# Attention and gated layer on one core: first pairs' scores on row halves of the array, leftover keys times V on row halves with one PSUM bank for each tile's output, and a re-tuned planner

## The chip, the core and the metric

The kernel runs on one core of a Trainium2 chip. The metric is the device time of one execution in microseconds (us). Most executions of one kernel agree within 0.3%.

## The reference, cut to what matters

```python
# q, k, v: [8 batches, 8 heads, 576 tokens, 64]; tau = 0.02
scores = scale * np.matmul(q, k.transpose(0, 1, 3, 2))
thresh = np.max(scores, axis=-1, keepdims=True) - tau
scores = np.where(scores >= thresh, scores, -1000000000.0)
attn = np.exp(scores - np.max(scores, axis=-1, keepdims=True))
attn = attn / (np.sum(attn, axis=-1, keepdims=True) + 1e-09)
x = np.matmul(attn, v)            # then [4608 tokens, 512]
gate = 1.0 / (1.0 + np.exp(-(x @ w_gate)))     # w_gate, w_val: [512, 1536]
out = (gate * (x @ w_val)) @ w_out             # w_out: [1536, 512]
```

## The kernel before

Two heads make a pair, and 32 visits (8 batches of 4 pairs) do the attention. 576 tokens are four tiles of 128 and 64 left over, so a visit has nine tiles of queries: four for each head and one (`l`) with the 64 leftover queries of both heads. For each tile, `tile_steps` (L580) makes the scores on TensorE in a PSUM tile `s` (L609), their negated maximum on VectorE (`st`, L616), the threshold (L625), the exponential on ScalarE (`p`, L630), and on VectorE the mask with the row sums (L633). `normalise` multiplies by the reciprocal on GpSimd (L667). `transpose` turns 4 x 128 keys of a tile by TensorE (`tp`, L678), and ScalarE copies them out (`pt`, L640). `leftover_keys` (L691) turns the 64 leftover keys of two tiles at once: `lk`, copied to `pl`, holds the leftover keys of the first tile in rows 0 to 63 and those of the second in rows 64 to 127.

`output` (L696) multiplies by V for two tiles at a time. One PSUM tile `av` takes both, 256 columns, and 64 more in the second output of a visit (the `l` tile). Head h writes rows h*64 to h*64+63, so two matmuls with 64 columns of weights each lie side by side in the array. For the leftover keys V stands twice in `vs`, once with zeros under it and once with zeros above it (blocks NJ and NJ+1), so that a 128-row matmul takes the one tile's half of `pl` alone. ScalarE copies `av` to `xf` (L721).

The first four visits (batch 0, `plain_scores`, L554) make their scores in full float32, one matmul of 128 rows for each half of the keys: the rows of both heads of K, and Q of one head with zeros in the rows of the other (`q0`). All later visits use a split in two parts that runs at the fast rate (`split_scores`, L515), for which halves are copied to `kd` and `qd` by DMA.

The rest is the gated layer ("moe"): matmuls `m` (L774) and `o` (L817) for the blocks of batches 0, 1 and 2, and after the attention the six blocks that are left, in pairs with sums of blocks (`qa`, `qb`, `qc` of L1016, `ra`, `rb`, `rc` of L1081; their inputs `xs_p` are made by L921, L924 and L929 from `xb`). Its weights are first converted (`convert`, L402): 24 blocks of the input weights and 12 of the output weights, each a DMA in, an absolute value on ScalarE, a clamp on GpSimd, three VectorE instructions (L442, L446, L452), a copy on ScalarE, a difference on GpSimd or VectorE (L470, L466), and a DMA out.

The order on every engine is worked out when the kernel is built, by a planner (`Plan.run`, L119). Each operation has an engine, a cost and a key, and an engine takes the ready operation with the smallest key. Attention has the number of its tile as key, conversions `CONV_IN` and `CONV_OUT` (start and step, in tiles), the gated layer's matmuls 1,000,000, so they fill what attention leaves. `LAG` is what the planner adds for an operation whose input comes from another engine. Tiles named `b` are four PSUM banks: `tp`, `lk` and `av` (class `att`) may hold three of them, and two once the gated layer has begun (`cap`, L372). An engine then runs its instructions in that order, and waits in place for what isn't ready. SyncE (SP) issues nearly all DMAs, in its order too.

Of the kernel before, what the change touches and what calls it, by code (L numbers as in the profile page):

```python
# [204 lines left out]
CONV_IN, CONV_OUT = (10, 1.5), (56, 3)  # L205
# [11 lines left out]
NPS = 4  # L217
# [15 lines left out]
THR_FIRST, THR_UNTIL, LK_UNTIL = "POOL", 72, 72  # L233
# [29 lines left out]
SUMS_IN, SUMS_OUT, SUM_KEY = {1: (0,), 2: (1,)}, {0: (0,), 1: (1,)}, 400  # L263
# [25 lines left out]
def kernel(  # L289
# [195 lines left out]
    class Visit:  # L485
# [17 lines left out]
        def prepare(self, lead):  # L503
# [50 lines left out]
        def plain_scores(self, key, n):  # L554
            b, hp, c0, c1 = self.b, self.hp, self.c0, self.c1
            WM = self.WM = c1 - c0
            kn = self.k1 = buf(("kn", "qn")[hp % 2], [P, SK], F32, f"kp{n}")
            op("SP", 1.2, key - 4, lambda: nc.sync.dma_start(out=kn.ap, in_=k[b, hp]), writes=[kn])
            W = 2 * WM + (2 * SL if self.with_left else 0)
            qn = self.q1 = buf("kd", [P, W], F32, f"qp{n}")  # L560

            heads = [(0,), (1,)] if n == "0_0" else [(0, 1)]
            for hs in heads:
                c = slice(hs[0] * WM, (hs[-1] + 1) * WM)
                op("SP", 0.9 * len(hs), key - 4, lambda hs=hs, c=c: nc.sync.dma_start(
                    out=qn.ap[:, c].rearrange("p (h c) -> p h c", h=len(hs)),
                    in_=q0[4 * b + hp, :, hs[0] : hs[-1] + 1, c0:c1],
                ), writes=[(qn, h) for h in hs])
# [3 lines left out]
            if len(heads) == 1:
                op("ACT", act(W), key, lambda: nc.scalar.activation(qn.ap, qn.ap, AF.Copy, scale=scale_t[:, 0:1]), writes=[qn])
                return
            for i, c in enumerate((slice(0, WM), slice(WM, 2 * WM), slice(2 * WM, W))):
                op("ACT", act(c.stop - c.start), key, lambda c=c: nc.scalar.activation(
                    qn.ap[:, c], qn.ap[:, c], AF.Copy, scale=scale_t[:, 0:1]
                ), writes=[(qn, i)])

    def tile_steps(vis, g, i, key):  # L580
# [24 lines left out]

        def scores():
            for m, (st, mv) in enumerate(steps):
                for c in range(2):
                    nc.tensor.matmul(  # L609
                        s.ap[:, c, :HALF], st(), mv(slice(k0 + c * HALF, k0 + (c + 1) * HALF)),  # L610
                        start=m == 0, stop=m == len(steps) - 1,
                    )

        op("PE", 0.98 if vis.plain_s else len(steps) * 2 * mm(HALF), key, scores, reads=reads, writes=[s], also=[g.p])
# [28 lines left out]
    class Group:  # L643
# [52 lines left out]
        def output(self, c, key):  # L696

            vis, pt, pl = self.vis, self.pt, self.pl
            last = self.tiles[0] != 0
            W = 2 * P + (SL if last else 0)  # L700
            av = buf("b", [P, W], F32, f"av{self.name}", "att")
            c0 = self.tiles[0] * P

            ms = [(0, 2 * P, j, lambda h, j=j: pt.ap[:, h, j]) for j in range(NJ)]
            ms += [(i * P, (i + 1) * P, NJ + i, lambda h: pl.ap[:, h]) for i in range(2)]
            if last:
                sl = lambda h: slice(h * SL, (h + 1) * SL)
                ms += [(2 * P, W, j, lambda h, j=j: c.pt.ap[:, 0, j, sl(h)]) for j in range(NJ)]
                ms += [(2 * P, W, NJ + 1, lambda h: c.pl.ap[:, 0, sl(h)])]

            def go():
                for i, (a, z, j, m) in enumerate(ms):
                    for h in range(2):
                        nc.tensor.matmul(  # L714
                            av.ap[h * D : (h + 1) * D, a:z], vis.vs.ap[:, j, h], m(h),
                            start=i == 0, stop=i == len(ms) - 1, skip_group_check=True,
                        )
# [506 lines left out]
def _laid_out(inputs):  # L1224
# [16 lines left out]
    first = _np.zeros((NPS, 2, d, 2, m), q.dtype)  # L1241
    pairs = q.reshape(b * h // 2, 2, d, s)
# [54 lines left out]
```

## Time and profile before

| what | us |
|---|---|
| median of 3 runs (1376.15, 1377.9, 1383.55) | 1377.9 |
| the profiled execution's own time | 1375.02 |
| its span, first to last instruction | 1373.2 |
| TensorE (PE) busy | 1332.4 (97%) |
| VectorE (DVE) busy | 982.3 (72%) |
| ScalarE (ACT) busy | 708.8 (52%) |
| GpSimd (POOL) busy | 639.0 (47%) |

The page has groups of instructions by line, `out<-in`, with the mean time of one; the views of the trace give the same for a stretch of time, the waits between engines, and the instructions in order of time. A float32 matmul stands there as two records. Three stages are to be told apart: the attention of batch 0 with the first conversions (up to about 123 us), attention with the gated layer's matmuls between (up to 837 us), and the gated layer alone.

### The profile page before, as it was taken

To read this page: it belongs to the slowest core of one execution; us is meant where nothing else is said; L and a number is where in the kernel's file an instruction comes from. 1 tells how busy PE (TensorE), PEld (TensorE's weight loads), DVE (VectorE), ACT (ScalarE), POOL (GpSimd) and SP (SyncE) were. 2 spreads that over 40 slices of the span, in tenths; PEclk is the share of its full clock that TensorE was granted. 3 is DMA by queue.
4 is the path that set the end of the run, shared out by engine and by line. 5 is a ranking of instruction groups with operands and counts; after the bars stand their busy time and mean duration, and the time that the engine had idled before them with its cause. 6 is when DMAs were issued, how large, how long until landed. Compare 5 with 4: busy or idle time off the path is not lost.

```text
span 1373.2 us, 23632 instructions
## 1 busy us (share of the span) xinstructions
PE 1332.4 (97%) x8276; PEld 1099.7 (80%) x8276; DVE 982.3 (72%) x2070; ACT 708.8 (52%) x1225; POOL 639.0 (47%) x681
## 2 busy tenths in 40 slices
PE   6888999999999999999999999999999999999998
PEld 5666888888788788888888887888888888888887
DVE  5898888777778787777878783456974569745584
ACT  5776766665566666566667663222532225322242
POOL 4888865884676685686787653011000110001100
PEclk9899999999999999999999999999999999999999
DMA  5769899888688779798879677766686566766664
GB/s 214 284 218 326 286 256 272 266 242 255 206 238 245 200 226 285 203 297 246 238 221 275 208 210 260 234 184 193 208 288 215 185 194 209 245 194 187 195 208 140
DMA packets 140292, 317.70 MB, mean 231 GB/s; under 512 B 22032, under 2 KB 49168, under 8 KB 140176
## 3 DMA queue, kind: packets, MB, share of 16 engines
q1 hardware_dynamic: 140032, 316.20, 75.0%
q8 instruction: 67, 1.10, 0.3%
q14 instruction: 49, 0.40, 0.1%
q10 hardware_dynamic: 144, 0.00, 0.0%
HBM read 210.24 MB, written 54.53 MB: 193 GB/s over the span
## 4 chain that ended last, share of the span: by engine, by line
PE 88%; DMA 4%; DVE 3%; issue 2%; POOL 2%; ACT 1%; SPq 0%; POOLq 0%; ACTq 0%; DVEq 0%
PE m L774 13%; PE qb L1016 11%; PE av L714 11%; PE s L609 10%; PE tp L678 7%; PE qc L1016 7%; PE qa L1016 7%; PE o L817 6%; PE rb L1081 5%; PE rc L1081 4%; PE ra L1081 4%; PE s_l L609 2%; DVE p L633 1%; PE tp_l L678 1%; PE lk L691 1%
## 5 line engine op out<-in xcount | busy, mean ns | idle before, releaser
L667 POOL TENSOR_SCALAR p<-p,zero_t,sm 128x576 f32<-128x576 f32 x256 | 215.1, 850 | 101.6 <-DVE sm L665 61.7
L616 DVE TENSOR_REDUCE st<-s 128x1 f32<-128x576 f32 x256 | 192.8, 754 | 84.0 <-PE s L609 82.6
L630 ACT ACTIVATE p<-s,st 128x576 f32<-128x576 f32 x256 | 190.5, 748 | 66.8 <-DVE st L616 56.3
L633 DVE SCALAR_TENSOR_TENSOR p<-s,st,p 128x576 f32<-128x576 f32 x256 | 206.4, 811 | 25.2 <-ACT p L630 19.0
L929 POOL TENSOR_TENSOR gA<-gA 128x512 f32<-128x512 f32 x18 | 24.2, 1343 | 417.1 <-DVE gA L995 417.1
L640 ACT COPY pt<-tp 128x512 f32<-128x512 f32 x256 | 148.6, 587 | 74.4 <-PE tp L678 73.4
L678 PE MATMUL tp<-ident,p 128*128 128x128 f32 x1024 | 157.0, 278 | 8.4 <-POOL p L667 8.1
L609 PE MATMUL s<-kd,qd 128*128 128x288 f32 x896 | 161.6, 305 | 3.5 <-DMA qd<-q 2.4
L774 PE MATMUL m<-x,wi 128*128 128x512 f32 x576 | 161.5, 405 | 0.0
L678 PEld LDWEIGHTS tp<-ident,p 128*128 128x128 f32 x1024 | 123.3, 142 | 34.6 <-POOL p L667 13.2
L609 PEld LDWEIGHTS s<-kd,qd 128*128 128x128 f32 x896 | 133.8, 189 | 14.4 <-DMA qd<-q 2.9
L714 PE MATMUL av<-pt,vs 128*64 128x256 f32 x1024 | 126.3, 385 | 0.7 <-ACT pt L640 0.7
L817 PE MATMUL o<-g,wo 128*128 128x512 f32 x432 | 120.1, 404 | 0.0
L953 DVE TENSOR_TENSOR qu<-qb,qp 128x512 f32<-128x512 f32 x72 | 49.8, 692 | 92.2 <-PE qb L1016 66.1
L774 PEld LDWEIGHTS m<-x,wi 128*128 128x128 f32 x576 | 98.8, 189 | 13.6
L1016 PE MATMUL qa<-xs_p,wa 128*128 128x512 f32 x432 | 109.6, 389 | 0.0
L714 PEld LDWEIGHTS av<-pt,vs 128*64 128x64 f32 x1024 | 68.4, 136 | 48.5 <-issue 7.7
L1016 PEld LDWEIGHTS qa<-xs_p,wa 128*128 128x128 f32 x432 | 81.1, 188 | 16.8
L817 PEld LDWEIGHTS o<-g,wo 128*128 128x128 f32 x432 | 74.5, 189 | 10.5
L921 ACT CAST gs_p<-gA 128x512 fp32r<-128x512 f32 x54 | 32.7, 620 | 77.4 <-DVE gA L995 41.5
L991 ACT ACTIVATE gA<-qa 128x512 f32<-128x512 f32 x18 | 10.8, 598 | 103.4 <-PE qa L1016 103.4
L640 ACT COPY xf<-av 128x256 f32<-128x256 f32 x64 | 25.6, 399 | 74.1 <-PE av L714 70.7
(151 smaller groups left out, 2687.5 us busy)
## 6 DMA issues: line engine op xcount, KB each, us to landing
kd<-k SPq DMA_DIRECT2D x112, 320.0 KB, 4.9
wi<-wid SPq DMA_DIRECT2D x48, 512.0 KB, 7.4
wo<-wod SPq DMA_DIRECT2D x36, 512.0 KB, 6.9
wa<-wid SPq DMA_DIRECT2D x36, 512.0 KB, 3.3
ws<-sid SPq DMA_DIRECT2D x36, 512.0 KB, 4.4
wt<-sid SPq DMA_DIRECT2D x36, 512.0 KB, 3.3
wo_p<-sod SPq DMA_DIRECT2D x36, 512.0 KB, 4.5
qd<-q SPq DMA_DIRECT2D x112, 128.0 KB, 3.4
```

Of the source, the lines that this page charges most:

```text
L609: nc.tensor.matmul(s.ap[:, c, :HALF], st(), mv(slice(k0 + c * HALF, k0 + (c + 1) * HALF)), start=m == 0, stop=m == len(steps) - 1,)
L616: op("DVE", 0.76, key, lambda: nc.vector.tensor_reduce(out=st.ap[:, 0:1], in_=sv(), axis=AX.XY, op=ALU.max, negate=True), reads=[s], write ...
L630: op("ACT", 0.74, key, lambda: nc.scalar.activation(p(), sv(), AF.Exp, bias=st.ap[:, 0:1], scale=1.0), reads=[s, (st, 0)], writes=[(g.p, i)])
L633: op("DVE", 0.9, key, lambda: nc.vector.scalar_tensor_tensor(out=p(), in0=sv(), scalar=st.ap[:, 1:2], in1=p(), op0=ALU.is_ge, op1=ALU.mult ...
L640: return op("ACT", act(n), key, lambda: nc.scalar.copy(dst(), src.ap), reads=[src], writes=[part])
L667: op("POOL", 0.9, key, lambda i=i: nc.gpsimd.tensor_scalar(out=p.ap[:, i * S : (i + 1) * S], in0=p.ap[:, i * S : (i + 1) * S], scalar1=zer ...
L678: nc.tensor.matmul(tp.ap[:, c, :], self.p.ap[:, o + c * P : o + (c + 1) * P], ident, is_transpose=True, start=c == 0, stop=c == NJ - 1, sk ...
L714: nc.tensor.matmul(av.ap[h * D : (h + 1) * D, a:z], vis.vs.ap[:, j, h], m(h), start=i == 0, stop=i == len(ms) - 1, skip_group_check=True,)
L774: nc.tensor.matmul(m.ap, wv[:, a, c * P : (c + 1) * P], xs[c].ap[:, z, c0:c1], start=e == 0, stop=e == 11,)
L817: nc.tensor.matmul(acc.ap, wv[:, f, a], g[fg * ND + f].ap[:, z], start=(fg, f, a, z) == (0, 0, 0, 0), stop=(fg, f, a, z) == (NFG - 1, ND - ...
L1016: nc.tensor.matmul(acc.ap, wv[:, y, (2 * h + c) * P : (2 * h + c + 1) * P], xt[prod][c].get()[:, z], start=e == 0 and prod in FIRST, stop= ...
L1081: nc.tensor.matmul(acc.ap, w.ap[:, e, c, y], gt[prod][2 * g + c].get()[:, z], start=m == 0 and g == 0 and prod in FIRST, stop=m == 5 and g ...
```

## The change

**Plain scores.** `q0` now holds, for each of the first four pairs and each head, the 64 rows of Q twice, in rows 0 to 63 and 64 to 127. A new input `k0` holds for each head the first half of the keys in rows 0 to 63 and the second half in rows 64 to 127. A score tile is two matmuls with 64 rows each, one in each row half of the array, writing the two banks of `s`. The `l` tile is four, each 64 rows by 64 columns. K lies in buffers of the tag `qd` instead of `kn` and `qn`.

**Output.** Each of the two tiles has a PSUM bank of its own (`avs`), so an output holds two banks `b`. The matmuls over 128 keys go by 128 columns a tile instead of 256 for both. The leftover keys of the first tile are a matmul on rows 0 to 63 and those of the second on rows 64 to 127; the zeros in V go (`vs` has NJ+1 blocks). ScalarE copies each bank by itself.

**The planner's numbers.** Conversions start at tile 2 with a step of 2.2 tiles, the lags change, and some small operations change engine: the threshold is on GpSimd up to tile 36 (before 72), the copy `pl` on ScalarE up to tile 108 (before 72), the differences of the input weights 18 to 23 on VectorE, those of the output weights on VectorE for block 10 alone (before 0, 4 and 8). The sums of weights have key 1000 instead of 400.

```diff
-CONV_IN, CONV_OUT = (10, 1.5), (56, 3)
+CONV_IN, CONV_OUT = (2, 2.2), (56, 3)
...
-LAG = {"PE": 0.4, "DVE": 0.2, "ACT": 0.2, "POOL": 0.2, "SP": 0.08}
+LAG = {"PE": 1.2, "DVE": 0.3, "ACT": 0.08, "POOL": 0.3, "SP": 0.08}
...
-            kn = self.k1 = buf(("kn", "qn")[hp % 2], [P, SK], F32, f"kp{n}")
...
+            self.k1 = [buf("qd", [P, HALF + SL], F32, f"kp{n}_{h}") for h in range(2)]
+            qn = self.q1 = buf("kd", [P, 2, S], F32, f"qp{n}")
...
+            heads = [(0, SM, 0, SL), (1, SM, SL, P)] if h is None else [(h, qt * P, 0, P)]
+            reads = [y for x, *_ in heads for y in ((vis.q1, x), vis.k1[x])]
...
+        def plain_scores():
+            for (x, c0, r0, r1), c in itertools.product(heads, range(2)):
+                rows = slice(c * D, (c + 1) * D)
+                nc.tensor.matmul(
+                    s.ap[r0:r1, c, :HALF], vis.q1.ap[rows, x, c0 : c0 + r1 - r0],
+                    vis.k1[x].ap[rows, kc : kc + HALF], start=True, stop=True, skip_group_check=True,
+                )
...
-            av = buf("b", [P, W], F32, f"av{self.name}", "att")
...
-            ms = [(0, 2 * P, j, lambda h, j=j: pt.ap[:, h, j]) for j in range(NJ)]
-            ms += [(i * P, (i + 1) * P, NJ + i, lambda h: pl.ap[:, h]) for i in range(2)]
+            avs = [buf("b", [P, P + SL * (last and i)], F32, f"av{self.name}{i}", "att") for i in range(2)]
+
+            ms = []
+            for j in range(NJ):
+                ms += [(i, 0, P, j, slice(0, P), lambda h, i=i, j=j: pt.ap[:, h, j, i * P : (i + 1) * P]) for i in range(2)]
+                if last:
+                    ms.append((1, P, P + SL, j, slice(0, P), lambda h, j=j: c.pt.ap[:, 0, j, h * SL : (h + 1) * SL]))
+            rows = [slice(i * D, (i + 1) * D) for i in range(2)]
+            ms += [(i, 0, P, NJ, rows[i], lambda h, i=i: pl.ap[rows[i], h]) for i in range(2)]
             if last:
...
+                ms.append((1, P, P + SL, NJ, rows[1], lambda h: c.pl.ap[rows[1], 0, h * SL : (h + 1) * SL]))
...
-            op("PE", AV_COST * W, key, go,
-               reads=[pt, pl] + ([c.pt, c.pl] if last else []) + [vis.vs], writes=[av], also=[vis.xf])
-            last_att[0] = copy(AV(vis.first), W, key, lambda: vis.xf.ap[:, c0 : c0 + W], av, (vis.xf, self.name))
+            op("PE", 2.85 if last else 2.28, key, go,
+               reads=[pt, pl] + ([c.pt, c.pl] if last else []) + [vis.vs], writes=avs, also=[vis.xf])
+            for i, av in enumerate(avs):
+                c0, W = self.tiles[i] * P, av.shape[1]
+                last_att[0] = copy(AV(vis.first), W, key, lambda av=av, c0=c0, W=W: vis.xf.ap[:, c0 : c0 + W], av,
+                                   (vis.xf, (self.name, i)))
```

**Where the instructions move.** SyncE's queue in the first stage, before: the queries `qn` of the first split visit (pair 0 of batch 1) and the copies `qd` that its scores read, behind the conversions of the first stage (`wr` raw weights in, `wid` converted weights out).

```order
60 L417 DMA wr_1_1225<-in_moe_w_val_dram 128x1024
61 L417 DMA wr_0_1239<-in_moe_w_gate_dram 128x1024
62 L525 DMA qn_0_1244<-in_q_dram 128x640
63 L475 DMA wid_1_120<-ws_1_1241 128x1024
64 L475 DMA wid_0_121<-ws_0_1254 128x1024
65 L546 DMA qd_0_0_1313<-q_0_1306 64x512
```

The same queue now, at its beginning; `kp` is the K of a plain visit, one DMA for each head.

```order
1 L564 DMA kp_0_0_176<-in_k_dram 128x352
2 L566 DMA qp_0_178<-in_q_dram 128x576 x2
3 L564 DMA kp_0_1_181<-in_k_dram 128x352
4 L514 DMA vs_0_183<-in_v_dram 128x640
5 L418 DMA wr_0_185<-in_moe_w_gate_dram 128x1024
...
15 L520 DMA kn_0_215<-in_k_dram 128x640
16 L526 DMA qn_0_219<-in_q_dram 128x640
...
52 L547 DMA qd_0_0_1012<-q_0_407 64x512
```

The queries of the first split visit have gone from row 62 to row 16, the first `qd` from row 65 to row 52, and the first weights to convert from row 9 to row 5.

VectorE at the beginning, before: reductions (`st`) and masks (`p`) of the first visit, and the first instruction of a conversion (`wb`).

```order
11 L616 TENSOR_REDUCE st_0_l_235<-s_0_l_226 128x1
12 L616 TENSOR_REDUCE st_0_020_240<-s_0_020_231 128x1
13 L633 SCALAR_TENSOR_TENSOR p_0_l_238,sm_0_l_257<-s_0_l_226,st_0_l_235,p_0_l_238 128x576
14 L665 RECIPROCAL sm_0_l_257<-sm_0_l_257 128x1
15 L633 SCALAR_TENSOR_TENSOR p_0_02_248,sm_0_02_268<-s_0_020_231,st_0_020_240,p_0_02_248 128x576
16 L616 TENSOR_REDUCE st_0_021_278<-s_0_021_264 128x1
17 L616 TENSOR_REDUCE st_0_100_289<-s_0_100_275 128x1
18 L442 TENSOR_SCALAR wb_0_297<-wa_0_273 128x512
```

The same place now.

```order
11 L443 TENSOR_SCALAR wb_0_244<-wa_0_224 128x512
12 L447 SCALAR_TENSOR_TENSOR wb_0_244<-wr_0_185,wb_0_244 128x512
13 L453 SCALAR_TENSOR_TENSOR wa_0_224<-wr_0_185,wb_0_244 128x512
14 L617 TENSOR_REDUCE st_0_l_252<-s_0_l_231 128x1
15 L617 TENSOR_REDUCE st_0_020_264<-s_0_020_240 128x1
16 L443 TENSOR_SCALAR wb_1_274<-wa_1_236 128x512
```

A whole conversion now stands ahead of the third tile's reduction. Up to the 36th tile's mask, the last of batch 0, VectorE has 19 conversions, before 20.

TensorE in the middle of the attention, before: an output (`av`) of a visit, with the transposes of the next tile behind it.

```order
895 L774 MATMUL m_11_1_0_6486<-x_0_1995,wi_11_1_6193 128x512
896 L774 MATMUL m_11_1_0_6486<-x_1_2995,wi_11_1_6193 128x512 x3
897 L714 MATMUL av_2_10_6527<-pt_2_00_6326,vs_2_5732 64x256 x8
898 L714 MATMUL av_2_10_6527<-pl_2_00_6346,vs_2_5732 64x128 x4
899 L678 MATMUL tp_2_120_6546<-ident,p_2_12_6464 128x128 x4
```

The end of such an output now.

```order
1047 L718 MATMUL av_3_100_5879<-pt_3_00_5624,vs_3_5056 64x128 x2
1048 L718 MATMUL av_3_101_5882<-pt_3_00_5624,vs_3_5056 64x128 x2
1049 L718 MATMUL av_3_100_5879<-pl_3_00_5653,vs_3_5056 64x128 x2
1050 L718 MATMUL av_3_101_5882<-pl_3_00_5653,vs_3_5056 64x128 x2
1051 L610 MATMUL s_0_l_5909<-k_0_5575,q_0_5646 128x288 x6
1052 L679 MATMUL tp_3_120_5919<-ident,p_3_12_5804 128x128 x4
```

Score matmuls (four or six of 288 columns) now stand between an output and the next transposes, which before followed it at once. Behind the last output of the attention, 54 matmuls `o` are left in the changed order ahead of the first `qa`; before, 80.

More of the change, by code (lines that the diff above doesn't have):

```diff
@@ L230, in AV @@
     return "ACT"
[L233 removed]
+THR_FIRST, THR_UNTIL, LK_UNTIL = "POOL", 36, 108
 def TP(g, i):
@@ L572, in plain_scores @@
[L572 to L578, printed above, removed]
+            pair = 4 * self.b + self.hp
@@ new lines, in plain_scores @@
+            self.k1 = [buf("qd", [P, HALF + SL], F32, f"kp{n}_{h}") for h in range(2)]
+            qn = self.q1 = buf("kd", [P, 2, S], F32, f"qp{n}")
+            for hs in [(0,), (1,)] if n == "0_0" else [(0, 1)]:
+                h = slice(hs[0], hs[-1] + 1)
+                for x in hs:
+                    op("SP", 0.7, key - 4 + x, lambda x=x: nc.sync.dma_start(out=self.k1[x].ap, in_=k0[pair, :, x]),
+                       writes=[self.k1[x]])
+                op("SP", 1.05 * len(hs), key - 4, lambda h=h: nc.sync.dma_start(out=qn.ap[:, h], in_=q0[pair, :, h]),
+                   writes=[(qn, x) for x in hs])
@@ L580, in tile_steps @@
+            for h in range(2):
+                op("ACT", act(S), key + h, lambda h=h: nc.scalar.activation(
+                    qn.ap[:, h], qn.ap[:, h], AF.Copy, scale=scale_t[:, 0:1]
+                ), writes=[(qn, h)])
     def tile_steps(vis, g, i, key):
@@ L721, in output @@
-            last_att[0] = copy(AV(vis.first), W, key, lambda: vis.xf.ap[:, c0 : c0 + W], av, (vis.xf, self.name))
+                            avs[i].ap[h * D : (h + 1) * D, a:z], vis.vs.ap[r, j, h], m(h),
+                            start=j == 0 and a == 0, stop=j == NJ and z == (P + SL if last and i else P),
+                            skip_group_check=True,
+                        )
+            op("PE", 2.85 if last else 2.28, key, go,
+               reads=[pt, pl] + ([c.pt, c.pl] if last else []) + [vis.vs], writes=avs, also=[vis.xf])
@@ L1240, in _laid_out @@
     given["q"] = _np.concatenate([q[..., :m], left.reshape(b, h // 2, 2 * d, -1)], axis=3)
-    first = _np.zeros((NPS, 2, d, 2, m), q.dtype)
-    pairs = q.reshape(b * h // 2, 2, d, s)
-    for i in range(2):
-        first[:, i, :, i] = pairs[:NPS, i, :, :m]
-    given["q0"] = first.reshape(NPS, 2 * d, 2, m)
-    given["k"] = _np.concatenate([k[..., m:], k], axis=3)
+    q0 = q.reshape(b * h // 2, 2, d, s)[:NPS].transpose(0, 2, 1, 3)
+    given["q0"] = _np.concatenate([q0, q0], axis=1)
+    k = given["k"] = _np.concatenate([k[..., m:], k], axis=3)
+    k0 = k.reshape(b * h // 2, 2, d, -1)[:NPS].transpose(0, 2, 1, 3)
+    given["k0"] = _np.concatenate([k0[..., : s // 2 + s - m], k0[..., s // 2 :]], axis=1)
     v = v.reshape(b, h // 2, 2, s, d).transpose(0, 1, 3, 2, 4)
     main = v[:, :, :m].reshape(b, h // 2, m // 128, 128, 2, d).transpose(0, 1, 3, 2, 4, 5)
-    last, zero = v[:, :, m:], _np.zeros_like(v[:, :, m:])
-    last = _np.stack([_np.concatenate(x, axis=2) for x in ((last, zero), (zero, last))], axis=3)
+    last = v[:, :, m:, None]
+    last = _np.concatenate([last, last], axis=2)
     for n in ("moe_w_gate", "moe_w_val"):
```

42 lines of the change are left out of this document (9 added, 33 removed).

## The prediction

> **What bounds the kernel now.** I read the page first, then the busy time by stage.
>
> ```profile
> span 1373.2 us, 23632 instructions
> ...
> PE 1332.4 (97%) x8276; PEld 1099.7 (80%) x8276; DVE 982.3 (72%) x2070; ACT 708.8 (52%) x1225; POOL 639.0 (47%) x681
> ```
>
> ```profile
> 0.00:10.70 10.70, 6.00 (x21) 5.03 (x22) 0.24 (x5) 2.91 (x4) 0.70 (x6) 1.00 0.74 259
> 10.70:116.00 105.30, 84.84 (x521) 60.66 (x521) 92.95 (x189) 76.65 (x143) 79.51 (x113) 0.94 0.73 252
> 116.00:130.00 14.00, 10.23 (x84) 7.72 (x82) 9.94 (x15) 8.32 (x16) 12.05 (x12) 1.00 0.85 283
> 130.00:170.00 40.00, 40.00 (x238) 33.33 (x238) 34.17 (x67) 29.57 (x55) 32.87 (x41) 1.00 0.90 292
> ...
> 470.00:570.00 100.00, 96.30 (x745) 80.60 (x744) 74.68 (x192) 61.63 (x104) 63.27 (x64) 1.00 0.84 243
> ...
> 837.00:1373.00 536.00, 532.38 (x2348) 440.62 (x2348) 332.04 (x495) 165.92 (x285) 54.26 (x40) 1.00 0.65 210
> ```
>
> The columns are the stretch, its length, busy time of PE, PEld, DVE, ACT and POOL, the granted TensorE clock, the DMA share and GB/s. From 130 us on PE is busy nearly all the time, whatever else runs: there an us less of TensorE work is an us less of the kernel, and a us in which PE waits is one more. Before 130 us it isn't so. From 10.7 to 116 us DVE is the fullest, 92.95 of 105.30 us, and PE waits for the softmax of batch 0, without which the gated layer can't begin. So the time is the end of that opening plus all PE work behind it, and the change is to be costed in two places: what ends the opening earlier or later, and what PE does behind it.
>
> **The opening.** What DVE does there, and what it waits for:
>
> ```profile
> L633 DVE SCALAR_TENSOR_TENSOR p<-s,st,p 128x576 f32<-128x576 f32 x32 | 25.8, 811 | 1.2 <-ACT p L630 1.0
> L616 DVE TENSOR_REDUCE st<-s 128x1 f32<-128x576 f32 x32 | 24.1, 753 | 12.1 <-PE s L609 12.0
> L442 DVE TENSOR_SCALAR wb<-wa 128x512 int32<-128x512 int32 x21 | 14.4, 685 | 0.1
> L446 DVE SCALAR_TENSOR_TENSOR wb<-wr,wb 128x512 int32<-128x512 int32 x20 | 13.8, 690 | 0.3
> L452 DVE SCALAR_TENSOR_TENSOR wa<-wr,wb 128x512 int32<-128x512 int32 x20 | 13.5, 677 | 0.2
> ```
>
> ```profile
> DVE st L616 <- PE s L609: 12.0, 13, 4.9
> DVE st_l L616 <- PE s_l L609: 2.7, 3, 1.3
> ```
>
> ```profile
> 10.71 0.76 DVE L616 TENSOR_REDUCE st<-s 128x1 f32<-128x576 f32 x1 [4.91 <-PE s L609]
> ```
>
> ```profile
> 8.38 4.21 PE L609 MATMUL s<-kp,qp 128*128 128x288 f32 x8 [3.35 <-ACT qp L576]
> ```
>
> The first tile's scores are four of the eight records in that last row, about 2 us; two row halves side by side make it half, 1 us less. Ahead of them the load of the first tile falls, by the shapes, from 128 x 640 values of K and 128 x 512 of Q to 128 x 352 and 128 x 576, or by 115 KB, some 0.4 us at the 259 GB/s of the first stretch; it shares the queues with other loads, so 0.3. The first reduction comes 1.3 us sooner. Behind it DVE waits 12.0 - 4.9 + 2.7 = 9.8 us more for scores. With scores of half the length, and conversions standing in the early gaps, I take half of it away, 4.9 us. One conversion fewer stands ahead of the 36th mask: 0.685 + 0.690 + 0.677 = 2.05 us. Sum: 1.3 + 4.9 + 2.05 = 8.25 us, taken as 8. Bounds: 13 if all those waits go. At the other end the opening gains nothing, if shorter scores only make PE idle longer (first rival). Work on ACT and POOL in this stretch (76.65 and 79.51 us of 105.30) is hardly changed and has room; without that room the gain would stop at what POOL leaves.
>
> Then comes the gap at the start of the gated layer:
>
> ```profile
> 123.52 2.44 PE L774 MATMUL m<-x,ws 128*128 128x512 f32 x10
> 128.39 0.79 PE L609 MATMUL s<-kd,qd 128*128 128x288 f32 x4 [2.43 <-DMA qd<-q]
> ```
>
> Ten `m` run from 123.52 us on, then PE waits for `qd`. Those copies now stand 13 rows sooner in SyncE's queue, their queries 46 rows sooner. The wait goes; late next is the transpose of the new `l` tile, which stands ahead of the first `m` and needs a softmax that starts one output earlier. I take 2 us off (0 to 2.4).
>
> **The outputs.** One output with its neighbours, in order of time (start, length until the last end, count):
>
> ```profile
> 498.62 0.86 PE L774 MATMUL m<-x,wi 128*128 128x512 f32 x3
> 499.40 1.95 PE L714 MATMUL av<-pt,vs 128*64 128x256 f32 x16
> 501.18 0.61 PE L714 MATMUL av<-pl,vs 128*64 128x128 f32 x8
> 501.62 0.64 PE L714 MATMUL av<-pt_l,vs 128*64 128x64 f32 x16
> 502.08 0.29 PE L714 MATMUL av<-pl_l,vs 128*64 128x64 f32 x4
> 502.30 0.66 PE L678 MATMUL tp<-ident,p 128*128 128x128 f32 x4
> ```
>
> ```profile
> L714 PE MATMUL av<-pt,vs x1024: 379/379/431, 37.1 to 835.5; 128*64 128x256 f32 x171
> ```
>
> ```profile
> 836.87 18.43 PE L817 MATMUL o<-g,wo 128*128 128x512 f32 x80
> ```
>
> Starts tell what each part occupies: 1.78 us for `pt`, 0.44 for the eight `pl` (four pairs of 0.11), 0.46 for `pt_l`, 0.22 for `pl_l` with the exit. The 80 `o` show 0.229 us for a 512-column matmul, so behind three of them the output could have begun at 498.62 + 0.69 = 499.31 and began 0.09 late, and its first records take up to 431 ns instead of 379. I read that as the price of going from whole-array weights (128*128) to 64 columns (128*64): about 0.15 us.
>
> After: `pt` is 16 pairs of 0.11 instead of eight of 0.22, the same; `pl` is two groups of four quadrants, 0.22 us instead of 0.44; but the array goes from 128*64 to quadrants once more, 0.15 us. Net 0.07 us less, less some 0.02 for twice the `pt` instructions: 0.05 us. Of the 64 outputs 56 lie behind the opening: 56 x 0.05 = 2.8, taken as 3 us. If that switch is free, 56 x 0.20 = 11 us. If quadrants of different rows don't run side by side, each output pays 0.17 us more, 10 us in all. I take 3: the switch is priced by the nearest row, the entry into this same output. [...]
>
> Twice as many PSUM copies go to ACT: a 128-column copy takes 0.27 us (the row below), so the pair takes some 0.15 us more than the one copy, on an engine busy 61.63 of 100 us in the middle. That costs nothing while ACT has that room.
>
> ```profile
> 109.35 0.27 ACT L640 COPY pl<-lk 128x128 f32<-128x128 f32 x1
> ```
>
> **The planner's numbers** do no work by themselves. Behind the opening PE's waits before were few:
>
> ```profile
> PE tp L678 <- POOL p L667: 6.6, 5, 2.2
> PE s L609 <- DMA qd<-q: 2.4, 1, 2.4
> ...
> PE lk L691 <- ACT pt L640: 0.3, 1, 0.3
> ```
>
> A lag of 1.2 us for PE puts each transpose further behind the softmax it needs, so some 3 of the 6.6 us should go (0 to 6.6). Against it stands a new wait: an output now needs both of attention's banks, and the next transpose needs one of them copied out. Score work of 0.53 us stands between. Its ends are 0 and the 0.5 us an output of the second rival below; the last row above, 0.3 us for all waits on ACT, is nearest to 0, so I set 56 x 0.05 = 3 us, and the two cancel.
>
> At the end of the attention PE has `o` work while the inputs of the next blocks are made:
>
> ```profile
> 847.02 1.11 DVE L924 TENSOR_TENSOR xs_p<-xb,xs_p 128x512 fp32r<-128x512 f32 x1 [13.37 <-ACT xs_p L921]
> 848.32 5.62 DVE L924 TENSOR_TENSOR xs_p<-xb,xs_p 128x512 fp32r<-128x512 f32 x6 [0.19 <-ACT xs_p L921]
> ```
>
> The first is ready at 848.13, 11.3 us behind the last output's end at 836.87; the fill falls from 80 to 54 matmuls, 54 x 0.229 = 12.4 us. It still covers the chain, by 1 us, so I count nothing; if the chain is late by two instructions of 0.7 us, it costs up to 1 us.
>
> **Sum.** 8 + 2 + 3 + 0 + 0 = 13 us off the profiled execution's 1375.0 us (span 1373.2 and 1.8 around it): 1362. The median of the runs is 2.9 us above the profiled time, so 1365.
>
> **The rivals.** *First: the opening gives little, because PE's clock falls.* In 10.7 to 116 us the granted clock averages 0.94, so about 0.06 x 105 x 2 = 12.6 us pass at half rate, although PE is busy 81% of it. Shorter scores leave PE more idle. With twice as much time at half rate, PE's work is late by up to 12.6 / 2 = 6.3 us, and DVE waits for it again: the opening gives 2 instead of 8, and the sum is 1365 + 6 = 1371; if the late work eats the rest too, 1373. For it: the clock did fall in this stretch, where PE's longest wait for the softmax was short (the last number of the row):
>
> ```profile
> PE s L609 <- DVE p L633: 14.3, 9, 2.6
> ```
>
> Against it: a half-length score at half rate is no longer than today's at full rate. [...] Chance 0.20, at 1371 to 1376.
>
> *Second, slower: two banks for each output make PE wait.* Behind each output the transpose needs ACT's copy of the first bank, and ACT may be in the middle of an exponential or a `pt` copy:
>
> ```profile
> L630 ACT ACTIVATE p<-s,st 128x576 f32<-128x576 f32 x256 | 190.5, 748 | 66.8 <-DVE st L616 56.3
> ```
>
> If the copy (0.27) regularly comes behind one such instruction (0.75), PE waits 0.75 + 0.27 - 0.53, some 0.5 us, 56 times: 28 us, and the kernel takes 1365 + 28 - 3 = 1390. It decides from 13 / 56 = 0.23 us an output. Against it: ACT is busy only 62% of the time, and before, with two banks for `tp` and `lk`, PE waited for ACT behind the opening for 0.3 us in all. 0.10. With row halves that don't run side by side (no gain in the scores, 10 us lost in the outputs: about 1383 to 1388) it is 0.12 for slower.
>
> *Third: the switch to quadrants is free.* The outputs give 11 instead of 3: 1357. For it: both are tilings by 64 columns. Against it: the 0.09 and the 431 ns above. 0.10.
>
> **How the numbers follow.** The forecast, 1365 with 1358 to 1371 of its own, has 0.58, the first rival 0.20, the slower ones 0.12, the third 0.10. What a measurement of this kernel can tell from no change is about 0.5%, 6.9 us: faster is under 1371. The forecast and the third make faster 0.68, the first same 0.20, slower 0.12. The range leaves out the slower cases and the far end of the opening's and the third's gain: 1351 to 1381.
>
> **What would show it.** Right: the first `m` at 112 to 118 us instead of 123.5, DVE's waits for plain scores down from 14.7 to below 8 us, outputs of 2.80 to 2.87 us instead of 2.90, no `qd` wait behind the opening, and PE busy at least 99% from there. Wrong: a first `m` later than 120 us; a clock below 0.90 in the opening; PE's waits for ACT behind the opening above 10 us in total, at the transposes behind outputs; or outputs longer than 2.90 us.

## The result, and the profile after

The changed kernel takes 1363.57 us (median of 4 runs, 1361.55 to 1365.29), beside 1380.35 us for the kernel before in the same comparison: a ratio of 0.988, with a 95% interval of 0.9845 to 0.9914, so 12 to 21 us faster. Its profiled execution takes 1363.83 us, 11.2 us less than that of before (1375.02), where 13 us were forecast. The before kernel's profiled execution is one of its fastest, so the medians lie further apart than the two profiles; what follows accounts for the 11.2 us.

The page after:

```profile
span 1362.0 us, 25859 instructions
...
PE 1324.5 (97%) x9316; PEld 1114.7 (82%) x9316; DVE 984.4 (72%) x2072; ACT 716.1 (53%) x1311; POOL 626.7 (46%) x659
```

Busy time by stage after, in the columns of the prediction (opening, its last part, attention with the gated layer's matmuls between, and the rest from the last output on):

```profile
0.00:9.50 9.50, 5.04 (x24) 3.96 (x24) 1.14 (x7) 2.83 (x4) 0.73 (x7) 0.96 0.73 245
9.50:106.00 96.50, 74.17 (x606) 50.96 (x607) 88.55 (x181) 74.85 (x147) 76.47 (x109) 0.82 0.78 264
106.00:117.60 11.60, 10.24 (x130) 8.48 (x129) 10.83 (x21) 8.61 (x21) 7.84 (x10) 0.92 0.94 325
117.60:830.10 712.50, 708.07 (x6238) 615.62 (x6236) 552.92 (x1371) 464.93 (x859) 487.87 (x496) 1.00 0.83 243
830.10:1362.00 531.90, 526.92 (x2326) 435.65 (x2322) 331.01 (x495) 164.91 (x285) 53.80 (x40) 1.00 0.64 209
```

The same two last stretches before, cut at its own first `m` (123.5) and the end of its last output (836.9):

```profile
123.50:836.90 713.40, 702.95 (x5329) 588.77 (x5327) 550.45 (x1373) 458.73 (x785) 497.56 (x516) 1.00 0.84 244
836.90:1373.20 536.30, 532.48 (x2350) 440.72 (x2348) 332.04 (x495) 165.93 (x285) 54.26 (x40) 1.00 0.65 210
```

The difference between length and PE's busy time is PE's idle time. The first `m` comes 5.9 us sooner. Between it and the last output PE idles 712.50 - 708.07 = 4.4 us instead of 10.5. Behind the last output it idles 5.0 instead of 3.8. PE's work behind the first `m` is 708.07 + 526.92 = 1235.0 us, and was 702.95 + 532.48 = 1235.4. So the 11.2 us are **5.9 (opening) + 6.0 (waits in the middle) - 1.2 (waits at the end) + 0.4 (work)**, 11.1 by the rounded terms. The middle stretch isn't shorter by itself because it holds more of the fill: 54 `o` are left behind the last output instead of 80.

**The opening after.** Three of DVE's groups up to 107.2 us, within the 36th mask:

```profile
L617 DVE TENSOR_REDUCE st<-s 128x1 f32<-128x576 f32 x32 | 23.7, 753 | 7.9 <-PE s L602 7.8
L447 DVE SCALAR_TENSOR_TENSOR wb<-wr,wb 128x512 int32<-128x512 int32 x19 | 13.1, 689 | 0.1
...
L617 DVE TENSOR_REDUCE st_l<-s_l 128x1 f32<-128x576 f32 x4 | 3.0, 748 | 0.6 <-PE s_l L602 0.6
```

The first reduction and the 36th mask after, and then that mask before, in order of time:

```profile
8.60 1.42 DVE L617 TENSOR_REDUCE st<-s 128x1 f32<-128x576 f32 x2 [3.67 <-PE s L602]
...
106.60 0.82 DVE L634 SCALAR_TENSOR_TENSOR p<-s,st,p 128x576 f32<-128x576 f32 x1
```

```profile
114.97 0.82 DVE L633 SCALAR_TENSOR_TENSOR p<-s,st,p 128x576 f32<-128x576 f32 x1 [0.59 <-ACT p L630]
```

DVE waits 7.8 + 0.6 = 8.4 us for plain scores instead of 14.7, and 19 conversions stand ahead of the mask instead of 20. That is 6.3 + 2.05 = 8.35 us, and the mask is 8.37 us sooner; two smaller differences cancel (DVE's first load lands 0.9 us sooner, and conversions wait 0.8 us for ScalarE, which they didn't before). But of these 8.4 us the first `m` keeps only 5.9. PE's last steps ahead of it:

```profile
116.10 0.77 PE L610 MATMUL s<-kd,qd 128*128 128x288 f32 x4 [0.99 <-DVE p_l L634]
117.14 0.66 PE L679 MATMUL tp_l<-ident,p_l 128*128 128x128 f32 x4 [0.27 <-POOL p_l L668]
117.63 0.27 PE L692 MATMUL lk_l<-ident,p_l 128*128 128x128 f32 x1
117.66 2.98 PE L782 MATMUL m<-x,ws 128*128 128x512 f32 x12
```

PE takes two score tiles of batch 1 and the `l` tile's transposes first; before the change they stood behind the first `m`. The waits are not what is lost: PE idles 1.3 us between the mask and the first `m`, and did so before. The 2.5 us are work, and most of it (some 1.6 us, by the starts of these 13 records) is then missing behind the first `m`.

**An output after**, in order of time; the first rows are a score tile behind `m` and one behind transposes, for comparison, and the last four one output with what is around it:

```profile
600.77 0.70 PE L610 MATMUL s<-kd,qd 128*128 128x288 f32 x4
601.31 1.09 PE L782 MATMUL m<-x,wi 128*128 128x512 f32 x4
...
606.29 0.77 PE L610 MATMUL s<-kd,qd 128*128 128x288 f32 x4
606.90 0.27 PE L692 MATMUL lk<-ident,p 128*128 128x128 f32 x1
...
728.02 1.97 PE L718 MATMUL av<-pt,vs 128*64 128x128 f32 x32
729.92 0.45 PE L718 MATMUL av<-pl,vs 64*64 64x128 f32 x8
730.30 0.79 PE L610 MATMUL s<-kd,qd 128*128 128x288 f32 x4
730.93 1.10 PE L782 MATMUL m<-x,wi 128*128 128x512 f32 x4
```

From the start of the output to the start of the next instruction it is 730.30 - 728.02 = 2.28 us. The median over the first outputs of all visits is 2.277, before 2.315; over the second ones 2.855, before 2.896. So an output is 0.04 us shorter. The scores behind it occupy 730.93 - 730.30 = 0.63 us, those at 600.77, behind `m`, only 0.54, and those at 606.29, behind transposes, 0.61.

**PE's waits** behind the opening after: the largest up to the last output, the one for `qd`, and the only one behind the last output:

```profile
PE tp L679 <- POOL p L668: 0.8, 1, 0.8
...
PE s L610 <- DMA qd<-q: 0.7, 1, 0.7
```

```profile
PE qb L1024 <- DVE qu L961: 1.2, 1, 1.2
```

Of the 6.6 us for `p` from GpSimd 0.8 are left, of the 2.4 us for `qd` 0.7, and no wait for ScalarE is among the larger ones.

### The profile page after: what moved, and what is told of

It is laid out like the page before. It is cut to its first block, busy times and chain, and to the rows that moved or that the text cites. A ratio compares the mean times of both kernels' runs of the same rounds, so it can differ in the third digit from the quotient of the medians.

```text
span 1362.0 us, 25859 instructions
## 1 busy us (share of the span) xinstructions
PE 1324.5 (97%) x9316; PEld 1114.7 (82%) x9316; DVE 984.4 (72%) x2072; ACT 716.1 (53%) x1311; POOL 626.7 (46%) x659
## 4 chain that ended last, share of the span: by engine, by line
PE 89%; DMA 3%; DVE 3%; ACT 2%; POOL 1%; issue 1%; SPq 0%; POOLq 0%; DVEq 0%; ACTq 0%
PE m L782 13%; PE av L718 11%; PE qb L1024 11%; PE s L610 9%; PE tp L679 7%; PE qa L1024 7%; PE qc L1024 7%; PE o L825 7%; PE rb L1089 5%; PE rc L1089 4%; PE ra L1089 4%; PE s_l L610 2%; PE lk L692 1%; DMA xp<-xf 1%; DVE p L634 1%
## 5 line engine op out<-in xcount | busy, mean ns | idle before, releaser
L610 PE MATMUL s<-kd,qd 128*128 128x288 f32 x896 | 167.6, 310 | 4.2 <-DVE p_l L634 1.3
L782 PE MATMUL m<-x,wi 128*128 128x512 f32 x576 | 164.3, 405 | 0.0
L679 PE MATMUL tp<-ident,p 128*128 128x128 f32 x1024 | 151.6, 279 | 3.8 <-POOL p L668 2.1
L718 PE MATMUL av<-pt,vs 128*64 128x128 f32 x2048 | 141.8, 282 | 0.1
L718 PEld LDWEIGHTS av<-pt,vs 128*64 128x64 f32 x2048 | 113.4, 141 | 22.9 <-issue 10.6
L782 PEld LDWEIGHTS m<-x,wi 128*128 128x128 f32 x576 | 98.2, 189 | 12.3 <-issue 0.2
L641 ACT COPY xf<-av 128x128 f32<-128x128 f32 (+1 forms) x128 | 29.5, 283 | 82.6 <-PE av L718 82.5
```

The lines of the kernel that those rows point to most:

```text
L610: nc.tensor.matmul(s.ap[:, c, :HALF], st(), mv(slice(kc + c * HALF, kc + (c + 1) * HALF)), start=m == 0, stop=m == len(steps) - 1,)
L641: return op("ACT", act(n), key, lambda: nc.scalar.copy(dst(), src.ap), reads=[src], writes=[part])
L679: nc.tensor.matmul(tp.ap[:, c, :], self.p.ap[:, o + c * P : o + (c + 1) * P], ident, is_transpose=True, start=c == 0, stop=c == NJ - 1, sk ...
L718: nc.tensor.matmul(avs[i].ap[h * D : (h + 1) * D, a:z], vis.vs.ap[r, j, h], m(h), start=j == 0 and a == 0, stop=j == NJ and z == (P + SL i ...
L782: nc.tensor.matmul(m.ap, wv[:, a, c * P : (c + 1) * P], xs[c].ap[:, z, c0:c1], start=e == 0, stop=e == 11,)
```

## The experiments

Three theories, beside "as predicted": that the planner's numbers alone brought the time; that fewer conversions, not shorter scores, brought the opening; and the first rival, that a lower clock costs part of the gain. "Mask" is the start of the 36th mask, "first `m`" its start, "idle" PE's idle time from there to the end of the last output, each in the profiled execution.

| kernel | median us (runs) | ratio to before, 95% | mask | first `m` | idle |
|---|---|---|---|---|---|
| before | 1380.35 (4) | | 114.97 | 123.52 | 10.5 |
| after | 1363.57 (4) | 0.988 [0.9845, 0.9914] | 106.60 | 117.66 | 4.4 |
| after, again | 1362.74 (6) | 0.9881 [0.9856, 0.9906] | 106.7 | 117.77 | 4.3 |
| numbers only | 1379.23 (12) | 1.0005 [0.9987, 1.0024] | 114.9 | 129.00 | 9.4 |
| old numbers | 1370.11 (6) | 0.9934 [0.991, 0.9959] | 107.1 | 120.56 | 8.4 |
| output as before | 1371.18 (8) | 0.9941 [0.9918, 0.9963] | 106.4 | 117.79 | 5.1 |
| scores as before | 1370.8 (6) | 0.9937 [0.9913, 0.996] | 113.3 | 125.03 | 5.3 |
| old lags | 1376.0 (12) | 0.9983 [0.996, 1.0005] | 108.2 | 122.55 | 5.3 |
| old `CONV_IN` | 1360.98 (6) | 0.9871 [0.9845, 0.9896] | 104.35 | 117.63 | 2.1 |
| scores twice | 1370.33 (6) | 0.9929 [0.9902, 0.9957] | 114.95 | 125.99 | 3.1 |
| leftovers on whole rows | 1361.81 (6) | 0.9877 [0.9851, 0.9903] | 101.8 | 112.81 | 3.0 |
| matmuls to keep the clock | 1389.22 (9) | 1.0074 [1.0051, 1.0098] | 129.2 | 140.25 | 4.7 |
| the same, old `CONV_IN` | 1392.61 (6) | 1.0099 [1.0071, 1.0126] | 135.4 | 149.04 | 1.7 |
| whole rows, old `CONV_IN` | 1367.74 (6) | 0.9924 [0.9899, 0.9949] | 108.0 | 122.46 | 1.7 |

### The planner's numbers alone

The kernel before with the new numbers and nothing else.

```diff
-CONV_IN, CONV_OUT = (10, 1.5), (56, 3)
+CONV_IN, CONV_OUT = (2, 2.2), (56, 3)
-LAG = {"PE": 0.4, "DVE": 0.2, "ACT": 0.2, "POOL": 0.2, "SP": 0.08}
+LAG = {"PE": 1.2, "DVE": 0.3, "ACT": 0.08, "POOL": 0.3, "SP": 0.08}
...
```

> The kernel before with the planner's new numbers alone (conversions, lags, engines of small operations, key of the sums); scores and outputs as before. Theory (numbers and row halves each give a part: one conversion less and fuller gaps in the opening, fewer PE waits behind it from the lag): 5 to 8 us less than before, about 1373, with the qd wait of 2.4 us at the first m still there, because K of the plain visits still lies in kn and qn. Rival A (the numbers do nearly all of it, row halves nothing): 13 to 17 us less, about 1365. Rival B (row halves do it, the numbers nothing): within 2 us of before.

1379.23 us, a ratio of 1.0005 [0.9987, 1.0024]: nothing. The mask is where it was before (114.9), so the mask's 8.4 us don't come from the numbers. Against what was expected, no wait for `qd` is left: PE has none from 114 us on.

### The row halves with the old numbers

After, with all five lines of numbers as before (the diff above the other way round).

> The changed kernel with the planner's old numbers. Theory: the row halves and the freed kn and qn buffers shorten the opening by some 4 to 6 us, the outputs give 2.2 us, PE's waits behind the opening stay at 7 to 10 us: about 1371 to 1374. Rival A (numbers do it): no more than 3 us less than before, 1377 or above. Rival B (row halves do it): about 1364 to 1367.

1370.11 us, ratio 0.9934 [0.991, 0.9959]. The mask is as early as after (107.1). PE idles 8.4 us in the middle instead of 4.4, and its three largest waits there are:

```profile
PE s L610 <- DMA qd<-q: 2.6, 3, 1.3
PE tp L679 <- POOL p L668: 2.4, 4, 0.9
PE s L610 <- DMA kd<-k: 2.3, 1, 2.3
```

So the numbers bring nothing alone and about 6.5 us (1370.11 - 1363.57) on top of the row halves: 2.9 us at the first `m`, just ahead of which PE waits 3.2 us for `qd` here, and 4.0 us of idle time. So it is the numbers that take the wait for `qd` away.

### One half of the change at a time

After, but with the output of before (one `av`, `pl` on whole rows):

```diff
-            avs = [buf("b", [P, P + SL * (last and i)], F32, f"av{self.name}{i}", "att") for i in range(2)]
+            av = buf("b", [P, W], F32, f"av{self.name}", "att")
...
```

> The changed kernel with the outputs of before (one bank for both tiles, zeros in V). Theory: 56 outputs behind the opening take 0.04 us more each, 2.2 us, so about 1366, and the median output is 2.90 us. Rival C (holding two banks costs PE more than the quadrants save): faster than the changed kernel, 1360 or below, with fewer PE waits.

After, but with the plain scores of before (128 rows, K in `kn` and `qn`):

```diff
-            self.k1 = [buf("qd", [P, HALF + SL], F32, f"kp{n}_{h}") for h in range(2)]
+            kn = self.k1 = buf(("kn", "qn")[hp % 2], [P, SK], F32, f"kp{n}")
...
```

> The changed kernel with the plain scores of before (128 rows with zeros, K in kn and qn). Theory: the opening ends 4 to 6 us later and the qd wait is back, so about 1368 to 1371, with the granted clock in the opening back at 0.9 or above. Rival A: within 2 us of the changed kernel. Rival B: 1374 or above.

1371.18 us without the output's change, 1370.8 without the scores'. Without the scores' change the opening is back where it was (mask 113.3, first `m` 125.03), and DVE waits 12.3 us for plain scores, 14.7 before:

```profile
DVE st L616 <- PE s L609: 12.3, 11, 4.9
```

That is the expected place. Without the output's change the opening is as after, though 20 conversions stand ahead of its mask (106.44 us), as before the change; DVE waits only 5.4 + 1.2 us for scores there:

```profile
L447 DVE SCALAR_TENSOR_TENSOR wb<-wr,wb 128x512 int32<-128x512 int32 x20 | 13.8, 692 | 0.3
```

So the early mask doesn't need one conversion fewer: VectorE does the additional one in time in which it waits otherwise. But 7.6 us are lost, not the 3 forecast. PE's end of the attention there shows where half of them go, in order of time:

```profile
839.14 1.64 PE L1017 MATMUL qa<-xs_p,wa 128*128 128x512 f32 x6
840.61 0.60 PE L679 MATMUL tp<-ident,p 128*128 128x128 f32 x4
...
841.08 1.64 PE L1017 MATMUL qc<-xs_p,ws 128*128 128x512 f32 x6
842.65 1.95 PE L715 MATMUL av<-pt,vs 128*64 128x256 f32 x16
```

```profile
PE qb L1017 <- ACT xs_p L922: 4.4, 1, 4.4
```

The fill had run out: no `o` is left behind the last output, `qa` and `qc` already stand between the last transposes, and then PE waits 5.0 us for the next inputs (the 4.4 us of this row and 0.6 for VectorE). With the output's change the planner keeps 54 `o` for that place. In the profiled executions that is 3.9 us more of idle time behind the last output. PE's work behind the first `m` is 2.9 us more (1237.9 instead of 1235.0), of which 2.0 are the outputs themselves by their starts, and its waits in the middle are 0.7 more. So half of what the output is worth here is what order the planner makes of it. That the fill ran out is shown; that its cause is the planner's cost for the longer output was not tried by itself.

### The lags, and the start of the conversions

After, with one line of before each:

```diff
-LAG = {"PE": 1.2, "DVE": 0.3, "ACT": 0.08, "POOL": 0.3, "SP": 0.08}
+LAG = {"PE": 0.4, "DVE": 0.2, "ACT": 0.2, "POOL": 0.2, "SP": 0.08}
```

> The changed kernel with the old lags alone (PE 0.4 instead of 1.2, and the other engines' old values). Theory (the lag of PE is what took waits out of PE behind the opening): idle time of PE between the first m and the last output back to 8 to 10 us from 4.4, about 1367 to 1369 us in all. Rival (those waits went with the buffers and banks of the row halves): within 2 us of the changed kernel's 1363.6.

```diff
-CONV_IN, CONV_OUT = (2, 2.2), (56, 3)
+CONV_IN, CONV_OUT = (10, 1.5), (56, 3)
```

> The changed kernel with the old start and step of the conversions alone (tile 10, step 1.5). Theory (the early conversions fill VectorE's gaps, and one conversion less stands ahead of the last mask): first m 2 to 4 us later than 117.7, about 1366 to 1368 us. Rival (the opening is set by PE's scores and their chain alone): first m within 1 us, within 2 us in all.

The lags: 1376.0 us, 12 us slower than after, 9.1 in the profiled execution. But not where the prediction's lag term had it: 4.9 us are in a later first `m` (122.55), 1.9 between it and the last output, and 2.3 behind that. Idle time in the middle rises by only 0.8 us, and GpSimd isn't its largest cause:

```profile
PE lk L692 <- ACT pt L641: 2.1, 1, 2.1
PE s L610 <- DMA qd<-q: 1.2, 1, 1.2
```

So the lag alone doesn't explain the 6 us of idle time that went.

The conversions: with the old start the mask is sooner still (104.35), and the whole takes 1360.98 us (1358.88 to 1364.78), which its few runs can't tell from after. Nineteen conversions stand ahead of the mask here too. The theory that an early start of the conversions made the opening shorter falls.

### Scores issued twice

After, with every plain score matmul made two times into the same place, in the same order, from the same buffers and loads:

```diff
-            for (x, c0, r0, r1), c in itertools.product(heads, range(2)):
+            for _, (x, c0, r0, r1), c in itertools.product(range(2), heads, range(2)):
```

> The changed kernel with each plain score tile's matmuls issued twice, into the same place; order, buffers and loads unchanged. Theory (the opening ends earlier because scores take PE half as long): first m at 122 to 125 us, the half-rate time in the opening down from 37 us towards 14, 1368 to 1371 us. Rival (freed buffers and earlier loads did it): first m at 117 to 119 us, within 2 us of the changed kernel.

The mask is back at 114.95 us, where it was before the change, with 19 conversions ahead of it and waits for scores doubled to 15.4 + 1.6 us:

```profile
L617 DVE TENSOR_REDUCE st<-s 128x1 f32<-128x576 f32 x32 | 24.1, 755 | 15.6 <-PE s L602 15.4
...
L617 DVE TENSOR_REDUCE st_l<-s_l 128x1 f32<-128x576 f32 x4 | 3.0, 750 | 1.6 <-PE s_l L602 1.6
```

```profile
114.95 0.81 DVE L634 SCALAR_TENSOR_TENSOR p<-s,st,p 128x576 f32<-128x576 f32 x1
```

The order is that of after and only the time of the scores differs (the granted clock is higher, 0.95 up to the mask), and the mask moves by 8.35 us. That the shorter scores end the opening sooner is shown. That the mask lands where it was before is in part chance: DVE waits 17.0 us for scores here and waited 14.7 before, with one conversion (2.05 us) more ahead. The total is 1370.33 us, 6.8 us more than after.

### The leftover keys on whole rows

After, with two banks for an output, but each `pl` matmul on 128 rows with zeros in V, as before:

```diff
-            ms += [(i, 0, P, NJ, rows[i], lambda h, i=i: pl.ap[rows[i], h]) for i in range(2)]
+            ms += [(i, 0, P, NJ + i, slice(0, P), lambda h: pl.ap[:, h]) for i in range(2)]
```

> The changed kernel with the leftover keys on all 128 rows again, V padded with zeros, and still one bank for each tile: no quadrants and no switch to them. Theory (two quadrant groups save 0.22 us and the switch costs 0.15): outputs of 2.91 to 2.93 us in place of 2.855, 3 to 4 us more in all, about 1367. Rival (the switch costs less or nothing): outputs of 3.0 us or more, and 8 us or more in all. Rival (the switch costs all that quadrants save): outputs of 2.86 or less.

The same with the old `CONV_IN`:

> Old start and step of the conversions, and the leftover keys on all 128 rows with zeros in V, one bank for each tile. Against the same with quadrants (1361 us): theory (56 outputs take 0.06 us more): 3 to 4 us more, 1364 to 1365 us. Rival (quadrants give nothing that the time shows): 1361 us or less.

The output itself goes as expected: 2.334 and 2.915 us instead of 2.277 and 2.855, so the quadrants save 0.06 us each. One of them, in order of time:

```profile
598.77 1.97 PE L717 MATMUL av<-pt,vs 128*64 128x128 f32 x32
600.57 0.61 PE L717 MATMUL av<-pl,vs 128*64 128x128 f32 x8
601.11 1.06 PE L610 MATMUL s_l<-k,q 128*128 128x288 f32 x6
```

PE's work from the first `m` to the last output is 710.93 us, 2.9 more than after's 708.07, near the 3.4 that 56 outputs of 0.06 us make:

```profile
9.50:101.80 92.30, 70.90 (x607) 48.38 (x607) 88.66 (x182) 74.97 (x148) 76.66 (x111) 0.85 0.84 281
...
112.80:826.70 713.90, 710.93 (x6238) 625.52 (x6236) 553.93 (x1371) 468.00 (x859) 486.07 (x496) 1.00 0.84 245
```

Yet the total isn't longer: 1361.81 us. The opening is 4.8 us shorter than after's. That it is not an effect of the whole rows is seen from the second kernel, in which the same edit makes the opening 4.8 us longer (122.46 beside 117.63 with the old `CONV_IN` alone) and the total 6.8 us longer. DVE's waits for plain scores go with it: 4.7 us here beside after's 8.4, and 8.1 in the second kernel beside 5.5. What decides these 5 us either way stays open. After run again has its mask within 0.1 us of the first time, so two executions show no such scatter.

### Matmuls that keep the clock up

Three more matmuls behind each plain score, into columns of the bank that nobody reads; in the second kernel with the old `CONV_IN`. After itself was run again beside them.

```diff
+            for _ in range(3):
+                nc.tensor.matmul(s.ap[:, 1, 384:512], ident, ident, start=True, stop=True, skip_group_check=True)
```

> The changed kernel with three more float32 matmuls of the identity by itself (128 columns) behind each plain score tile, into columns of the same PSUM tile that nothing reads, so that TensorE is idle less. Theory (half rate costs the opening some us): less than 12 us at half rate in the opening, the 36th mask at 104 us or sooner instead of 106.6, about 1358 to 1361 us. Rival (half rate costs nothing, as a half-length score at half rate is no longer than the old one): the 36th mask at 106 us or later and 1363 us or more, by what the extra matmuls take.

> The same extra matmuls with the old start and step of the conversions (tile 10, step 1.5), which by themselves gave 1361 us. Theory (half rate costs the opening): 1355 to 1359 us, and faster than both kernels. Rival: 1361 us or more.

> The changed kernel as it is, once more. Theory (the opening depends on where the half-rate stretches of TensorE's clock fall, which differs from run to run): the first m may lie some us away from 117.7, with the time at half rate in the opening away from 37 us in the same direction; median 1361 to 1365 us. Rival (the opening is the same in each run, and the kernel with whole rows for the leftover keys had an opening of its own): first m within 1 us of 117.7.

This failed as a test of the clock. The reduction waits for the last of the added matmuls (0.17 us in the second row), though it reads none of their columns. PE and then DVE in order of time:

```profile
59.60 0.76 PE L602 MATMUL s<-kp,qp 64*128 64x288 f32 x4 [1.63 <-DVE p L636]
60.29 0.94 PE L607 MATMUL s<-ident 128*128 128x128 f32 x6
```

```profile
61.26 0.76 DVE L619 TENSOR_REDUCE st<-s 128x1 f32<-128x576 f32 x1 [0.17 <-PE s L607]
```

So each tile's scores became about 0.87 us longer for DVE, and the mask moved to 129.2 us; the clock in the opening rose only to 0.92. As a dose of longer scores it agrees with the scores issued twice: 1389.22 and 1392.61 us. What the clock costs it can't tell.

## Why the prediction was right

The forecast of 1365 us held, and faster was its likeliest side. That the mechanism of the opening was right is shown; that the total came so near is in part luck. The terms 8 + 2 + 3 + 0 + 0 came as 5.9 + 2 + 0.4 + 4 - 1.2: the first and the third fell short, the fourth brought what the sum had at nothing, and the misses cancel. So do two others: the profiled execution took 1.8 us more than the sum said, and the 2.9 us put on for the median weren't there (1363.57 beside 1363.83). By its steps:

- **The opening, 8 us: the cause and the three parts held, a following step was missed.** The first reduction came 2.1 us sooner (10.71 to 8.60; 1.3 forecast, 1.24 of it in DVE's wait), the other waits for plain scores fell from 9.8 to 4.7 us (4.9 forecast as a half), and one conversion fewer stood ahead. The reason given for the half, conversions in the early gaps, is not borne out: the old start of the conversions leaves still shorter waits. And the same shorter scores go with waits of 4.7 to 9.8 us in the kernels above, so that it came to just the half is luck. The price of the scores was too low as well: from its first start to its last end a tile takes 0.76 us at the full clock where it took 1.14 (rows below), not half. What failed is that the first `m` would follow the mask as before: it comes 11.1 us behind it instead of 8.6, behind more of batch 1's scores and the `l` tile's transposes that the step on `qd` had named as late next. So 5.9 us instead of 8, with some 1.6 us of work already done that stood behind before.
- **The wait for `qd`, 2 us: gone as forecast.** The largest wait for `qd` that is left anywhere behind is 0.7 us.
- **The outputs, 3 us: priced nearly rightly, and not found again in PE's work.** 0.04 us an output against 0.05, so 56 x 0.04 = 2.2 us. The `pl` matmuls start 1.90 us behind the output's start (729.92 - 728.02), and 1.80 us where they stay on whole rows (600.57 - 598.77, shown above), so the switch makes them 0.10 us late (0.15 in the forecast), and some of their records last longer than the least one (the columns are the least, median and longest duration in ns):

```profile
L718 PE MATMUL av<-pl,vs x512: 269/295/390, 37.1 to 829.8; 64*64 64x128 f32 x171
```

  So the switch is not free and the third rival falls; what the array does at it isn't shown. But a score tile and not a transpose now stands behind an output: behind 52 of the 56 outputs that follow the first `m`, where it was 8 before, with a transpose behind 44. By the medians of the starts, the first record of a score behind an output takes 0.237 us until the next, behind an `m` 0.131; of a transpose 0.165 and 0.108. That is 52 x 0.106 - (44 x 0.057 + 8 x 0.106) = 2.2 us more, as much as the outputs save. PE's work behind the first `m` is in fact only 0.4 us less, although 1.6 us of it now stand ahead. But that the place behind the outputs takes the gain isn't shown. Behind transposes, where many scores stood before, that first record takes 0.217 us. And in the kernel without the output's change, with the same records ahead of the first `m`, a transpose or `lk` stands behind 53 of the 56 outputs; beside it, after's scores take 2.4 us more by their starts, its transposes and `lk` 2.4 us less, and the 2.0 us of the outputs are saved. Where the order loses what the outputs save against before stays open.
- **The planner's lag against the two banks, 0: mis-sized.** No waits for ScalarE's copy came (the second rival falls with them), and PE's idle time in the middle fell by 6.0 us, of which `qd` was forecast: 3.6 to 4 us more than the term had. The cause of it is settled only in part: it needs both the row halves and the new numbers (8.4 us of idle time with the old numbers, 9.4 with the new numbers alone), and the old lags alone bring back only 0.8 us. So the step that had PE's lag take some 3 of the 6.6 us for GpSimd isn't borne out: that wait is 1.0 us with the old lags, and 2.4 with all the old numbers.
- **The end of the attention, 0 to 1 us lost: 1.2.** The fill of 54 `o` covered the chain to the first `qa`, and the wait came a step later, at `qb`.
- **The first rival: the lower clock came, its price didn't.** The granted clock in the opening is 0.82 instead of 0.94, lower than the 0.90 that was named as a sign of being wrong, and still DVE's waits fell by as much as forecast. The reason given, that a half-length score at half rate is no longer than the old one, doesn't hold. These are a score tile before, at a granted clock of 1.00, and two after, the first at 0.50 (the clock from 77.0 to 87.3 us), the second at 1.00:

```profile
99.14 1.14 PE L609 MATMUL s<-kp,qp 128*128 128x288 f32 x4
```

```profile
77.00 1.32 PE L602 MATMUL s<-kp,qp 64*128 64x288 f32 x4 [0.27 <-DVE p L634]
...
97.78 0.76 PE L602 MATMUL s<-kp,qp 64*128 64x288 f32 x4 [1.49 <-DVE p L634]
```

  At half rate the new tile is the longer one; but 22 of the 32 (without the `l` tiles) ran wholly at the full clock. What brings the clock down isn't shown. After, it was 0.82 with PE busy 74.17 of 96.50 us and no wait longer than the 2.9 us of the row below; before, 0.94 with 84.84 of 105.30 us and no wait longer than 2.6:

```profile
PE s L602 <- DVE p_l L634: 2.9, 1, 2.9
```

  What the lower clock still costs there stays open: the kernel made for it moved DVE's waits too.

## What to carry to other kernels

Where one engine sets the end of a stage, price a faster operation elsewhere by the waits that it ends on that engine, and show it by issuing the operation twice in the same order: the wait must come back. Follow the gain to the next step that must start, since an order made by a planner can put other work into the gap. Where the order is planned, compare the work of its neighbours on the same records as well, and try the parts together and alone: here the numbers gave 0 us alone and 6.5 us with the rest, and the parts don't add up.

## What the runs showed of the hardware that wasn't expected

- Quadrants of 64 by 64 run four side by side: the eight `pl` records of an output start in two groups of four, 6 to 7 ns apart within a group and 140 ns between the groups. They take 730.30 - 729.92 = 0.38 us with the exit, where eight on whole rows take 601.11 - 600.57 = 0.54.
- The row halves take the plain scores of the opening from 41.3 to 26.3 us of PE's time (without the `l` tiles), not to half. They do run side by side: at the full clock their records start in pairs 7 ns apart, a pair every 0.24 us, where single records started every 0.24 us before, and two tiles back to back take 1.24 us instead of 2.18. But a single tile takes 0.76 instead of 1.14 (rows above), as the first pair takes 0.35 us until the next and the last record ends 0.40 us behind its start. And more of them run at half rate (34 records last over 0.6 us, where 23 did), and a record lasts 530 ns in the mean instead of 471:

```profile
L602 PE MATMUL s<-kp,qp 64*128 64x288 f32 x120 | 26.3, 530 | 17.4 <-DVE p L634 13.2 <-DVE p_l L634 2.9 <-PE s L602 0.7
```

```profile
L609 PE MATMUL s<-kp,qp 128*128 128x288 f32 x124 | 41.3, 471 | 16.1 <-DVE p L633 14.3 <-PE lk L691 0.9 <-DVE p_l L633 0.7
```

  The rows are those of after (9.5 to 106 us) and of before (10.7 to 116 us); PE's idle time ahead of the scores, the wait for the softmax, hardly changes (17.4 and 16.1 us).
- What a group costs depends on what stands ahead of it: the first record of a score takes 0.131 us until the next behind `m`, 0.217 behind transposes and 0.237 behind an output's 64-column matmuls; that of a transpose 0.108 behind `m` and 0.165 behind an output.
- An opening of some 118 us, in which two engines wait for each other by turns, moved by 5 us either way with the same edit (the leftover keys on whole rows), while after run again stayed within 0.1 us. In both pairs the longer opening has the lower granted clock (0.82 beside 0.85; 0.83 beside 0.86 with the old `CONV_IN`), which shows no cause.
